# The branch to the general assignment moves from the middle of the program to its end, and redoes the second MoE there

## The chip, the cores and the metric

The kernel runs on one core of one Trainium2 chip. The metric is the device time of one execution in microseconds. The core's engines are PE (TensorE matmuls; PEld is its weight load), DVE (VectorE), ACT (ScalarE), POOL (GpSimd) and SP (SyncE, which issues most DMAs); each runs its own instruction list, and they wait for each other by semaphores. A q behind a name (DVEq) is the engine's sequencer, which also takes the branches.

## What is computed

Three layers follow one another on 1,536 tokens of 512 numbers: attention, an MoE in which every expert sees every token with gates from Sinkhorn sweeps, and a second MoE in which each token goes to one expert:

```python
def _moe2_ref(x, w_gate, w1, w2):
    N, D = x.shape                       # 1536, 512
    E = w_gate.shape[1]                  # 8
    cap = N // E                         # 192
    logits = x @ w_gate
    order = np.argsort(-logits.flatten())
    assigned = -np.ones(N, dtype=np.int64)
    counts = np.zeros(E, dtype=np.int64)
    for idx in order:
        tok, e = (int(idx) // E, int(idx) % E)
        if assigned[tok] >= 0 or counts[e] >= cap:
            continue
        assigned[tok] = e
        counts[e] += 1
    out = np.zeros((N, D), dtype=np.float32)
    for e in range(E):
        mask = assigned == e
        out[mask] = np.maximum(x[mask] @ w1[e], 0.0) @ w2[e]
    return out
```

## The kernel before

Tokens lie on the 128 partitions in twelve tiles. Every product is made of parts: a weight is split into a high and a low half (w1hs and w1ls, w2hs and w2ls; ACT copies the high half, L891, DVE subtracts it for the low one, L889), an activation too (hh and hl). SP loads raw weights (w1r at L867, w2r at L872) into a few buffers, and a load waits until the split has freed its buffer.

The order on each engine is written by a planner, `Sched`: a task has an engine, a cost, dependencies, a priority and buffers or PSUM banks that it takes and gives back; `sch.run()` emits the instructions in the planned order, and the hardware then waits for data alone.

Of the first MoE the last sweeps matter here. `make_gate2` works out the second MoE's gate from the weights of the first: SP loads the gate matrix (wgb) and, block by block, w2 of the last expert (w2f, L1478, two buffers); DVE multiplies them (L1483, 64 products that write the tile junk and keep a sum). Beside it, `zero_rows` (L1466 to L1468) has SP write zeros from junk, which POOL has cleared (L1470), to the first 192 rows of xs_d, the DRAM tensor that the tokens are sorted into.

`make_routing` then assigns tokens by rounds, on DVE, PE and ACT, gives every token a row number (pos) and a flag, flagi, that is 1 if the rounds did not reach the assignment of the reference. With the inputs timed here it is 0. `scatter(t)` on POOL (L1910, L1911) writes the token rows of tile t to xs_d by an indirect DMA, 128 rows of 513 words (512 numbers and the token's index). Ten tiles go first, eight of them from acc, two from accl; the last two tiles, which the first MoE finishes last, go later, and expert 0, whose rows are read before that, gets them by one-hot matmuls instead (slot and hot, L1986 and L1990; the matmuls are L2028).

`general()` stands between the ten scatters and everything that reads xs_d:

```python
            rv = nc.values_load(flagi[0:1, 0:1], min_val=0, max_val=1)
            with tc.If(rv > 0):
                for rnd in range(E - 1):
                    choose(rnd == 0)
                    exact_rank()
```

All five engines load the flag (L1819) and branch (L1820) over the exact assignment and a new set of scatters. It is at that place on each engine's list, so what stands behind it, deferred matmuls of the first MoE (L1090), splits and loads, comes after the branch on its engine.

The second MoE then goes expert by expert (`make_rows`, `make_tr`, `make_step2`): SP loads the expert's rows (xs, L1953), PE transposes them (L2021), multiplies by w1 (L2062 to L2064) and by w2 (L2106 to L2115), ACT and DVE make ya and yb (L2128 to L2135), and `put` (L2138, L2139) on POOL writes them to the output by an indirect DMA with the token's index; there are 16 puts. L206 is a planned filler matmul, L2265 the end of the program.

Of the kernel before, what the change touches and what calls it, by code (L numbers as in the profile page):

```python
# [22 lines left out]
def tile_attention_moe_moe(ctx, tc, q, k, v, n_sink, window, wg1, w1a, w2a, wg2, w1b, w2b, out):  # L23
    nc = tc.nc
# [1418 lines left out]
    def make_gate2():  # L1443
# [3 lines left out]
        def g0():  # L1447
            pool = gctx.enter_context(tc.tile_pool(name="gp", bufs=1, side="right", reuse_waits="tile"))
            gp.update(pool=pool, wgb=pool.tile([P, E, DM], F32, name="wgb"), junk=pool.tile([P, DM], F32, name="junk"),
                      wgt=pool.tile([E, DM], F32, name="wgt"), wgd=dram.tile([E, DM], F32, name="wgd"))  # L1450
            for c in range(DC):
                nc.tensor.transpose(bank["wgt"][:E, c * P:(c + 1) * P], wgr[:, 1, c, :], ident)
# [13 lines left out]
        def zero_rows():  # L1466
            nc.sync.dma_start(xs_d[0:P, 0:DM], gp["junk"])
            nc.sync.dma_start(xs_d[P:cap, 0:DM], gp["junk"][:cap - P])  # L1468

        x = task("POOL", 0.5, lambda: nc.gpsimd.memset(gp["junk"], 0.0), deps=[wgb], prio=pr)  # L1470
# [144 lines left out]
    def make_routing():  # L1615
        pr = -1000.0

        def open_():
            gctx.close()
            pool = rctx.enter_context(tc.tile_pool(name="rt", bufs=1, side="right", reuse_waits="tile"))  # L1620
            for nm, shape, dt in (("V", [P, NT, E], F32), ("A", [P, NT, E], F32), ("K", [P, NT], F32), ("OH", [P, NT, E], F32),
# [5 lines left out]
                                  ("Kr", [P, NT, P], F32), ("S3", [P, 3, NT, E], F32), ("R3", [P, 3, E], F32), ("tv", [P, 3, E], F32),  # L1627
                                  ("T1", [P, NT, E], F32), ("T2", [P, NT, E], F32), ("mxd", [P, NT], F32),
                                  ("Gd", [P, NT, P], BF), ("Gq", [P, P], BF),
# [187 lines left out]
        def general():  # L1817

            rv = nc.values_load(flagi[0:1, 0:1], min_val=0, max_val=1)  # L1819
            with tc.If(rv > 0):  # L1820
                for rnd in range(E - 1):
                    choose(rnd == 0)
                    exact_rank()
                choose(False)
                p = spare()
                rank(p)
                place(p)
                earlier = [o.ins.name for o in sc]
                sc.clear()
                z = rt["Kr"].rearrange("p a b -> p (a b)")[:, :DM]  # L1830
                nc.vector.memset(z, 0.0)
                fill = [nc.gpsimd.dma_start(xs_d[0:P, 0:DM], z), nc.gpsimd.dma_start(xs_d[P:cap, 0:DM], z[:cap - P])]
                for t in range(NE):
                    scatter(t)
                for a, b in [(f, o) for f in fill for o in earlier] + [(sc[0], f.ins.name) for f in fill]:
                    tc.add_manual_dep(a.ins, b, mybir.DependencyInfo(mybir.DependencyClass.Sync, mybir.DependencyReason.DATA),
                                      reason="the rows are written again")

# [59 lines left out]
        return task("X", 0.0, general, deps=SCT + [flag], name="general")  # L1898

    def make_last_scatters():  # L1900
        for t in range(NE, NT):
            SCT.append(task("POOL", 1.1, lambda t=t: scatter(t), deps=[gen, CB[t]] + LDX[0], prio=t, name="scatter"))
# [41 lines left out]
    def make_rows(e, sw):  # L1944
# [11 lines left out]
        LDX[e].append(task("SP", 1.1, ldx, deps=SCT + [sw, gen], prio=v_two(8 * e - 26.0) - (500 if e == 0 else 0), use=[XSH[e]], name=f"xs{e}"))  # L1956

    def make_tr(e):
# [22 lines left out]
        if e == 0:  # L1981
# [11 lines left out]
            hots = {t: task("DVE", 0.2, lambda t=t: hot(t), deps=[h0, gen], prio=-900.0, name="hot") for t in range(NE, NT)}  # L1993
# [53 lines left out]
    def make_step2(s):  # L2047
# [89 lines left out]
        def put(j):  # L2137
# [3 lines left out]
                in_=tl["ya" if j == 0 else "yb"], in_offset=None)  # L2141
# [75 lines left out]
    def more_banks2():  # L2217
        sch.names.extend(("hp0", "hp1"))
        sch.banks.extend([gen.end] * 2)
# [5 lines left out]
    gen = make_routing()  # L2225
    task("X", 0.0, more_banks2, deps=[gen], name="banks")
    sw2 = make_switch2(DEF + [gen])
# [8 lines left out]
    assert not sch.held and made[0] == len(loads)  # L2236

# [32 lines left out]
```

## Time and profile before

| | us |
|---|---|
| median of 3 runs | 1367.23 (1365.68 to 1368.32) |
| the profiled execution's own time | 1365.38 |
| its span, first to last instruction | 1363.6 |
| PE busy in it | 1347.4 (99%) |
| DVE, ACT, POOL busy | 918.0, 610.9, 97.7 |
| mean granted clock of TensorE | 0.998 |

The rows further down come from this one execution; times are us from its first instruction unless marked ns. In a timeline row stand the start, the duration, the engine, the line, the operation, what it writes and reads, and in brackets the idle time of the engine ahead of it with what ended it; a row may group several instructions (x2). In the waits, the engine that waited stands left of the arrow, what it waited for right of it. The time from a DMA's issue to its landing is counted from the issuing instruction to the last byte's arrival. The granted clock (PEclk) is 1.00 at full speed.

### The profile page before, as it was taken

Reading aid. Unit: us, or ns where it says so; the run is one execution under the profiler, and the core shown is the slowest. Engines: PE = TensorE matmul, PEld = TensorE weight load, DVE = VectorE, ACT = ScalarE, POOL = GpSimd, SP = SyncE. Lnnn points to the kernel's source line nnn. Section 1 sums busy time; section 2 is a strip of 40 time slices with the busy share of each in tenths; the row PEclk is TensorE's granted clock in tenths of the full one; section 3 lists DMA queues with packets and bytes.
Section 4 is the critical chain, followed back from the end, with each engine's and each line's share of the span. In section 5 each row is a group of like instructions: output and inputs, shape, how many; then the busy total and the mean of one; then the engine's idle time right before and its main releaser. Section 6 shows DMA issues by size and latency. Waiting matters only on the chain. (4 is left out here: it accounts for less than half of the span.)

```text
span 1363.6 us, 22464 instructions
## 1 busy us (share of the span) xinstructions
PE 1347.4 (99%) x8301; PEld 1171.6 (86%) x8301; DVE 918.0 (67%) x2445; ACT 610.9 (45%) x1543; POOL 97.7 (7%) x238
## 2 busy tenths in 40 slices
PE   8999999999999999999999999999999999899998
PEld 8988888999988888899989888888887777688887
DVE  8877767866555555646364655449889968578885
ACT  7867753734333332424242333331133354267874
POOL 3111110000000000000000000000001023410111
PEclk9999999999999999999999999999999999999999
DMA  7322101201010101011020201061020010478772
GB/s 171 102 63 51 46 17 54 72 22 63 11 52 17 47 19 44 31 32 52 11 62 1 63 4 59 24 216 36 16 93 16 1 47 17 119 231 255 259 225 99
DMA packets 98529, 96.23 MB, mean 71 GB/s; under 512 B 42088, under 2 KB 76392, under 8 KB 98288
## 3 DMA queue, kind: packets, MB, share of 16 engines
q1 hardware_dynamic: 96432, 88.46, 21.8%
q0 software_dynamic: 1984, 6.30, 1.5%
q8 instruction: 66, 1.08, 0.3%
q14 instruction: 47, 0.39, 0.1%
HBM read 86.47 MB, written 8.28 MB: 69 GB/s over the span
## 5 line engine op out<-in xcount | busy, mean ns | idle before, releaser
L1366 ACT ACTIVATE hh<-c 128x256 fp32r<-128x256 f32 x180 | 74.8, 416 | 124.5 <-DVE c L1333 111.0
L1155 PE MATMUL hp<-xp,w1hs 128*128 128x512 f32 x384 | 120.8, 395 | 0.0
L1333 DVE TENSOR_TENSOR c<-hp,cp 128x256 f32<-128x256 f32 x120 | 50.9, 424 | 96.1 <-PE hp L1308 92.7
L1397 PE MATMUL o<-w2ls,hh 128*128 128x512 f32 x240 | 95.0, 396 | 0.0
L1397 PE MATMUL o<-w2hs,hh 128*128 128x512 f32 x240 | 94.4, 393 | 0.0
L1397 PE MATMUL o<-w2hs,hl 128*128 128x512 f32 x240 | 94.4, 393 | 0.0
L1308 PE MATMUL hp<-xp,w1hs 128*128 128x256 f32 x480 | 88.1, 282 | 0.0
L1155 PEld LDWEIGHTS hp<-xp,w1hs 128*128 128x128 f32 x384 | 69.5, 188 | 14.9
L1369 DVE SCALAR_TENSOR_TENSOR hl<-c,hh 128x256 fp32r<-128x256 f32 x180 | 74.5, 419 | 10.4 <-ACT hh L1366 7.8
L1308 PEld LDWEIGHTS hp<-xp,w1hs 128*128 128x128 f32 x480 | 76.6, 188 | 4.6
L1155 PE MATMUL hp<-xp,w1ls 128*128 128x512 f32 x192 | 75.8, 395 | 0.0
L1059 PE MATMUL hp<-xp,w1hs 128*128 128x256 f32 x384 | 74.5, 288 | 0.0
L1090 PE MATMUL o<-w2hs,hh 128*128 128x512 f32 x168 | 68.7, 409 | 4.2 <-PEq L1820 4.2
L1366 ACT ACTIVATE hh<-hp 128x256 fp32r<-128x256 f32 x60 | 23.1, 384 | 107.1 <-PE hp L1308 107.1
L1572 POOL TENSOR_TENSOR hl<-h,hh 128x256 fp32r<-128x256 f32 x15 | 12.9, 863 | 795.8 <-ACT hh L1569 792.1
L1325 ACT ACTIVATE cu<-hp 128x256 f32<-128x256 f32 x60 | 23.0, 383 | 102.7 <-PE hp L1308 102.6
L1308 PE MATMUL hp<-xp,w1ls 128*128 128x256 f32 x240 | 67.5, 281 | 0.0
L1090 PE MATMUL o<-w2ls,hh 128*128 128x512 f32 x168 | 67.0, 399 | 0.0
L1090 PE MATMUL o<-w2hs,hl 128*128 128x512 f32 x168 | 66.5, 396 | 0.0
L1369 DVE SCALAR_TENSOR_TENSOR hl<-hp,hh 128x256 fp32r<-128x256 f32 x60 | 25.4, 424 | 58.7 <-ACT hh L1366 58.4
L889 DVE TENSOR_TENSOR w1ls<-w1r,w1hs 128x512 fp32r<-128x512 f32 x84 | 57.1, 686 | 9.8 <-ACT w1hs L891 9.0
L889 DVE TENSOR_TENSOR w2ls<-w2r,w2hs 128x512 fp32r<-128x512 f32 x84 | 56.0, 683 | 9.3 <-DVEq L1820 6.4
(497 smaller groups left out, 4017.7 us busy)
## 6 DMA issues: line engine op xcount, KB each, us to landing
wr<-in_moe_w_dram SPq DMA_DIRECT2D x44, 512.0 KB, 3.6
w1r<-in_moe_w_dram SPq DMA_DIRECT2D x42, 512.0 KB, 4.6
w2r<-in_moe_w_dram SPq DMA_DIRECT2D x42, 512.0 KB, 4.2
xs<-xs_d SPq DMA_DIRECT2D x14, 256.5 KB, 4.2
nk<-in_k_dram SPq DMA_DIRECT2D x12, 256.0 KB, 3.3
nq<-in_q_dram SPq DMA_DIRECT2D x12, 256.0 KB, 3.8
nv<-in_v_dram SPq DMA_DIRECT2D x12, 256.0 KB, 3.2
wgb<-wgd SPq DMA_DIRECT2D x1, 2048.0 KB, 8.9
```

The source lines that it names most:

```text
L889: (nc.gpsimd if eng == "POOL" else nc.vector).tensor_tensor(lo[:, c], r[:, c], f32(hi[:, c]), op=OP.subtract)
L1059: nc.tensor.matmul(p, a, b, start=(c == 0 and j == 0), stop=(c == DC - 1 and j == 2), skip_group_check=True)
L1090: nc.tensor.matmul(OUTP[g, j], a_, b_, start=(first and i == 0), stop=(last and i == 2), skip_group_check=True)
L1155: nc.tensor.matmul(HS[k, 0].rearrange("p a b -> p (a b)"), a, b, start=(c == 0 and j == 0), stop=(c == DC - 1 and j == 2), skip_group_chec ...
L1308: nc.tensor.matmul(st[bk], l_[:, c], r_[:, c], start=(start and c == 0 and j == 0), stop=(c == 1 and j == 2), skip_group_check=True)
L1325: act(st[key], st[bk], AF.Copy)
L1333: tt(st[out], st[bk], st[key], op=OP.add)
L1366: act(hh, st[key], AF.Relu)
L1369: nc.vector.scalar_tensor_tensor(HT[i, f, t][1], st[key], 0.0, f32(HT[i, f, t][0]), op0=OP.max, op1=OP.subtract)
L1397: nc.tensor.matmul(OUTP[g, j % GT], a_, b_, start=(first and f == 0 and z == 0), stop=(last and f == 1 and z == 2), skip_group_check=True)
L1572: (nc.gpsimd if eng == "POOL" else nc.vector).tensor_tensor(HT[s][1], h32_of(g, fc), f32(HT[s][0]), op=OP.subtract)
```

## The change

`general()` is no longer a task of the plan. It is called once, after `sch.run()`, behind the last instruction of every engine, and its body now does the exact assignment, twelve scatters, and the whole second MoE again in a plain loop. The rest of the program no longer depends on it: the last scatters, xs and hot depend on `placed` (the row numbers), and the banks hp0 and hp1 come back to the planner when the first MoE's last H32 tasks end instead of when the branch does. Since the second MoE now runs ahead of the branch even where the rounds failed, rows of xs_d that no token was sorted into must be harmless: all 1,536 rows are filled from a tile of their own (zero) with zeros and the index N, in twelve DMAs, and `put` has a bounds check that drops rows with the index N.

```diff
+                      wgt=pool.tile([E, DM], F32, name="wgt"), wgd=dram.tile([E, DM], F32, name="wgd"),
+                      zero=pool.tile([P, XW], F32, name="zero"))
...
         def zero_rows():
-            nc.sync.dma_start(xs_d[0:P, 0:DM], gp["junk"])
-            nc.sync.dma_start(xs_d[P:cap, 0:DM], gp["junk"][:cap - P])
-
-        x = task("POOL", 0.5, lambda: nc.gpsimd.memset(gp["junk"], 0.0), deps=[wgb], prio=pr)
+            for j in range(NT):
+                nc.sync.dma_start(xs_d[j * P:(j + 1) * P, :], gp["zero"])
+
+        def zero():
+            nc.gpsimd.memset(gp["zero"][:, :DM], 0.0)
+            nc.gpsimd.memset(gp["zero"][:, DM:], float(N))
+
+        x = task("POOL", 0.5, zero, deps=[wgb], prio=pr)
...
-        return task("X", 0.0, general, deps=SCT + [flag], name="general")
+        rt.update(choose=choose, exact_rank=exact_rank, rank=rank, place=place, spare=spare)
+        return place_, flag
 
     def make_last_scatters():
         for t in range(NE, NT):
-            SCT.append(task("POOL", 1.1, lambda t=t: scatter(t), deps=[gen, CB[t]] + LDX[0], prio=t, name="scatter"))
+            SCT.append(task("POOL", 1.1, lambda t=t: scatter(t), deps=[placed, CB[t]] + LDX[0], prio=t, name="scatter"))
+
+    def general():
+
+        choose, exact_rank, spare = rt["choose"], rt["exact_rank"], rt["spare"]
...
+        rv = nc.values_load(flagi[0:1, 0:1], min_val=0, max_val=1)
+        with tc.If(rv > 0):
...
+            for rnd in range(E - 1):
+                choose(rnd == 0)
+                exact_rank()
...
+            for t in range(NT):
+                scatter(t)
+            for e in range(E):
...
-        LDX[e].append(task("SP", 1.1, ldx, deps=SCT + [sw, gen], prio=v_two(8 * e - 26.0) - (500 if e == 0 else 0), use=[XSH[e]], name=f"xs{e}"))
+        LDX[e].append(task("SP", 1.1, ldx, deps=SCT + [sw, placed], prio=v_two(8 * e - 26.0) - (500 if e == 0 else 0), use=[XSH[e]], name=f"xs{e}"))
...
-                in_=tl["ya" if j == 0 else "yb"], in_offset=None)
+                in_=tl["ya" if j == 0 else "yb"], in_offset=None, bounds_check=N - 1, oob_is_err=False)
...
-        sch.banks.extend([gen.end] * 2)
+        sch.banks.extend([max(x.end for x in B_HP)] * 2)
...
     sch.run()
     assert not sch.held and made[0] == len(loads)
+    general()
```

On every engine the order of the other instructions is the same as before, apart from the names of PSUM banks in the routing and the zero rows. What moves is the load of the flag, the branch, and the body that is jumped over. The body has, in rows of the instruction order, before and now: PE about 2,300 and 900, DVE 407 and 771, ACT 23 and 312, POOL 25 and 61, SP 2 and 83.

**At the old place of the branch, SP.** Before (w1r and w2r are raw weights, xs the rows of expert 0):

```order
L867 DMA w1r<-in_moe_w_dram 128x4x256 x5
L1819 TENSOR_LOAD flagi
L1819 ISA x2
L1820 COMPARE_AND_BRANCH
L1820 UNCONDITIONAL_BRANCH x2
L872 DMA w2r<-in_moe_w_dram 128x2x512 x2
L1953 DMA xs_14661<-xs_d 128x512
L1953 DMA xs_14663<-xs_d 64x512
L872 DMA w2r<-in_moe_w_dram 128x2x512 x2
```

Now the w2r load that stood behind the branch follows the last w1r load directly:

```order
L867 DMA w1r<-in_moe_w_dram 128x4x256 x5
L872 DMA w2r<-in_moe_w_dram 128x2x512 x2
L2021 DMA xs_12972<-xs_d 128x512
L2021 DMA xs_12974<-xs_d 64x512
L872 DMA w2r<-in_moe_w_dram 128x2x512 x2
```

The flag's load and the branch are gone from this place; the order of the loads is kept.

**At the old place of the branch, PE.** Before (o and av are PSUM banks, hh and hl the halves of an activation of the first MoE; L1871 is the first row of the body):

```order
L1090 MATMUL av<-w2ls_130,hh 128x512
L1090 MATMUL o_12879<-w2hs_129,hl 128x512
L1090 MATMUL av<-w2hs_129,hl 128x512
L1819 TENSOR_LOAD flagi
L1820 COMPARE_AND_BRANCH
L1871 MATMUL hp_12938<-ident,rK 128x128 x4
L1871 MATMUL hp_12944<-ident,rK 128x128 x4
L1871 MATMUL hp_12950<-ident,rK 128x128 x4
```

Now the matmuls that stood behind the body follow directly, in the same order, into banks of other names:

```order
L1090 MATMUL side_12889<-w2ls_130,hh 128x512
L1090 MATMUL hp_12884<-w2hs_129,hl 128x512
L1090 MATMUL side_12889<-w2hs_129,hl 128x512
L1090 MATMUL hp_12884<-w2hs_129,hh 128x512
L1090 MATMUL side_12889<-w2hs_129,hh 128x512
L1090 MATMUL hp_12884<-w2ls_130,hh 128x512
L1090 MATMUL side_12889<-w2ls_130,hh 128x512
```

On DVE it is the same: behind the two hl (L1572) there stood the flag's load and the branch, and now the split of w2r into w2ls (L889) and the next two hl follow.

**At the end, DVE.** Now (yb is the last tile of the second MoE, and ended DVE's list before; L1899 is the first row of the new body):

```order
L2156 SCALAR_TENSOR_TENSOR hs<-sm,hs 128x128
L2157 SCALAR_TENSOR_TENSOR hs<-sm,hs 128x64
L2203 TENSOR_TENSOR yb<-av,yb 64x512
L1897 TENSOR_LOAD flagi
L1898 COMPARE_AND_BRANCH
L1899 CAST gonesb<-ones 128x128
L1900 CAST gbefb<-before 128x128
```

The flag's load and the branch stand behind yb, and likewise behind the last instruction of every other engine.

**At the zero rows, SP.** Before:

```order
L1478 DMA w2f<-in_moe_w_dram 128x512
L1467 DMA xs_d<-junk 128x512
L1468 DMA xs_d<-junk 64x512
L1478 DMA w2f<-in_moe_w_dram 128x512
L872 DMA w2r<-in_moe_w_dram 128x2x512
L867 DMA w1r<-in_moe_w_dram 128x4x256
```

Now:

```order
L1483 DMA w2f<-in_moe_w_dram 128x512
L1469 DMA xs_d<-zero 128x513 x12
L1483 DMA w2f<-in_moe_w_dram 128x512
L872 DMA w2r<-in_moe_w_dram 128x2x512
L867 DMA w1r<-in_moe_w_dram 128x4x256
```

The twelve DMAs stand where the two stood, ahead of the second w2f load.

## Rows read from the trace of the kernel before

**Rows 1.** Waits of PE, longest first: us in total, times, longest.
```profile
PE o L1090 <- PEq L1820: 4.2, 1, 4.2
```

**Rows 2.** Line L1820, the branch, by engine: duration ns, first and last start.
```profile
L1820 ACTq COMPARE_BRANCH  x1: 50/50/50, 1181.1 to 1181.1; - x1
L1820 ACTq EVENT_SEMAPHORE  x1: 17/17/17, 1181.6 to 1181.6; - x1
L1820 DVEq COMPARE_BRANCH  x1: 72/72/72, 1182.1 to 1182.1; - x1
L1820 DVEq EVENT_SEMAPHORE  x1: 21/21/21, 1187.8 to 1187.8; - x1
```

**Rows 3.** Line L1819, the load of the flag, on DVE.
```profile
L1819 DVEq TENSOR_LOAD <-flagi x1: 803/803/803, 1181.2 to 1181.2; - x1
```

**Rows 4.** Timeline of PE at the branch: start us, us, what; idle before it.
```profile
1182.04 0.39 PE L1090 MATMUL av<-w2hs,hl 128*128 128x512 f32 x1
...
1186.66 0.47 PE L1090 MATMUL o<-w2hs,hh 128*128 128x512 f32 x1 [4.23 <-PEq L1820]
...
1190.62 0.39 PE L1090 MATMUL o<-w2hs,hl 128*128 128x512 f32 x1
...
1195.29 1.52 PE L2021 MATMUL side<-ident,xs 128*128 128x128 f32 x8
```

**Rows 5.** Windows: busy us (xcount) of PE, PEld, DVE, ACT, POOL; PEclk, DMA share, GB/s.
```profile
1186.66:1190.62 3.96, 3.96 (x11) 3.11 (x12) 2.62 (x7) 1.46 (x3) 0.33 (x2) 0.57 0.10 19
...
1201.80:1355.70 153.90, 153.25 (x887) 135.11 (x886) 125.58 (x342) 110.62 (x268) 18.46 (x28) 1.00 0.70 224
```

**Rows 6.** Timeline of SP around the branch.
```profile
1173.46 16.22 SPq L872 DMA_DIRECT2D w2r<-in_moe_w_dram  x2
1189.79 0.98 SPq L1953 DMA_DIRECT2D xs<-xs_d  x2
```

**Rows 7.** Timeline of POOL: the tenth scatter, and what waits for its landing.
```profile
1180.99 0.96 POOL L1911 DMA_INDIRECT xs_d<-accl,pos  x1 [0.21 <-POOLq L1820]
1189.63 0.29 POOL L1986 IOTA slot<- 128x192 f32 x1 [7.68 <-DMA xs_d<-acc,pos]
```

**Rows 8.** DMA issues, us to landing: first four scatters, all scatters, then the row loads.
```profile
xs_d<-acc,pos POOLq DMA_INDIRECT x4, 5.1
...
DMA to landing us min/median/max: 3.8/5.9/9.0
...
DMA to landing us min/median/max: 2.7/3.0/4.9
```

**Rows 9.** Windows, columns as in the fifth group: loads, and the scatters.
```profile
915.00:920.00 5.00, 5.00 (x23) 4.02 (x22) 2.25 (x7) 0.58 (x2) 0.00 (x0) 1.00 0.94 281
...
1170.00:1182.30 12.30, 12.30 (x55) 9.71 (x53) 5.91 (x18) 4.50 (x11) 10.03 (x18) 1.00 0.84 218
```

**Rows 10.** SP's second load of w2f: its issue, and its us to landing.
```profile
905.53 0.79 SPq L1478 DMA_DIRECT2D w2f<-in_moe_w_dram  x1
...
w2f<-in_moe_w_dram SPq DMA_DIRECT2D x1, 256.0 KB, 12.7
```

**Rows 11.** Timeline of DVE at the gate products (L1483) and next to them.
```profile
918.17 0.69 DVE L1483 SCALAR_TENSOR_TENSOR junk<-w2f,wgb 128x512 f32<-128x512 f32 x1 [2.23 <-DMA xs_d<-junk]
...
924.58 0.69 DVE L1483 SCALAR_TENSOR_TENSOR junk<-w2f,wgb 128x512 f32<-128x512 f32 x1
...
927.40 0.75 DVE L1178 SCALAR_TENSOR_TENSOR hl<-hp,hh 128x256 fp32r<-128x256 f32 x2
```

**Rows 12.** Timeline of PE: the matmul that first takes that hl.
```profile
931.20 0.39 PE L1090 MATMUL o<-w2hs,hl 128*128 128x512 f32 x1
```

**Rows 13.** Timeline of DVE and POOL at the end, and POOL's last drain (L2265).
```profile
1357.99 0.68 DVE L2135 TENSOR_TENSOR yb<-o,yb 64x512 f32<-64x512 f32 x1 [2.87 <-ACT yb L2132]
1358.95 0.90 POOL L2139 DMA_INDIRECT out_dram<-yb,idx  x1 [0.28 <-DVE yb L2135]
...
L2265 POOLq DRAIN  x3: 40/113/4022, 1358.7 to 1363.3; - x3
```

More of the change, by code (lines that the diff above doesn't have):

```diff
@@ L1449, in g0 @@
             gp.update(pool=pool, wgb=pool.tile([P, E, DM], F32, name="wgb"), junk=pool.tile([P, DM], F32, name="junk"),
-                      wgt=pool.tile([E, DM], F32, name="wgt"), wgd=dram.tile([E, DM], F32, name="wgd"))
+                      wgt=pool.tile([E, DM], F32, name="wgt"), wgd=dram.tile([E, DM], F32, name="wgd"),
+                      zero=pool.tile([P, XW], F32, name="zero"))
             for c in range(DC):
@@ L1626, in open_ @@
                                   ("mk", [P, E], F32), ("fl", [P, 4], F32), ("posf", [P, NT], F32),
-                                  ("Kr", [P, NT, P], F32), ("S3", [P, 3, NT, E], F32), ("R3", [P, 3, E], F32), ("tv", [P, 3, E], F32),
-                                  ("T1", [P, NT, E], F32), ("T2", [P, NT, E], F32), ("mxd", [P, NT], F32),
-                                  ("Gd", [P, NT, P], BF), ("Gq", [P, P], BF),
+                                  ("T1", [P, NT, E], F32), ("T2", [P, NT, E], F32),
                                   ("bte", [P, NT, E], F32), ("far", [P, NT], F32)):
@@ L1815, in make_routing @@
         place_ = task("DVE", 0.9, lambda: place(bank["rk"]), deps=[y], prio=pr - 1, rel="rk")
[L1817 to L1837, printed above, removed]
         sp_n = [0]
@@ L1992, in make_tr @@
             h0 = task("POOL", 0.3, hot0, deps=[sw2], prio=-900.0)
-            hots = {t: task("DVE", 0.2, lambda t=t: hot(t), deps=[h0, gen], prio=-900.0, name="hot") for t in range(NE, NT)}
+            hots = {t: task("DVE", 0.2, lambda t=t: hot(t), deps=[h0, placed], prio=-900.0, name="hot") for t in range(NE, NT)}
         for c2 in range(DC // 2):
@@ L2224, in tile_attention_moe_moe @@
         make_deferred(q_)
-    gen = make_routing()
-    task("X", 0.0, more_banks2, deps=[gen], name="banks")
-    sw2 = make_switch2(DEF + [gen])
+    placed, flag = make_routing()
+    B_HP = list(H32.values())
+    task("X", 0.0, more_banks2, deps=B_HP, name="banks")
+    sw2 = make_switch2(DEF + [placed, flag])
     for e in range(E):
```

74 lines of the change are left out of this document (added).

## The prediction, made before the changed kernel ran

> **What bounds the kernel now.** PE is busy for nearly the whole span (the table above), so whatever makes the program shorter must take idle or slow time from PE, or time from the tail behind its last matmul. I read the list of PE's waits first. Its longest is at the branch of L1820, 4.2 us, once [rows 1]. The view of that line by engine tells who stood there: DVE branches at 1182.1 and goes on at 1187.8, while ACT branches at 1181.1 and goes on at 1181.6 [rows 2]. Both skip the same body, of which DVE has 407 rows in the instruction order and ACT 23. So the stall goes with the length of what is jumped over; it isn't the load of the flag, which took DVE 0.8 us of its own ahead of the branch [rows 3]. PE's timeline shows the whole price [rows 4], the windows show that PE came back at a granted clock of 0.57, the 1.2 GHz level for most of it, for 3.96 us, and that the second MoE behind it is PE's again: 153.25 us busy of 153.90 [rows 5]. A microsecond saved ahead of it therefore reaches the end, unless PE waits for something else on the way.
>
> **The branch leaves the middle: −6.0 us.** From the last matmul ahead of the branch to the next one are 1186.66 − 1182.04 = 4.62 us [rows 4]. From 1190.62 to 1195.29, 20 matmuls take 4.67 us, 0.2335 us each, so 4.39 us of the 4.62 are idle. The ten matmuls from 1186.66 to 1190.62 take 3.96 us instead of 2.34: 1.62 us of slow clock. Together 6.0. PE can then begin the transposes of expert 0's rows (L2021 of before) at 1195.29 − 6.0 = 1189.3.
>
> **What is late next: +1.0 us.** These transposes read xs of expert 0, which SP loads from xs_d behind the tenth scatter's landing; that dependency stays. Before, the tenth scatter was issued at 1180.99, and POOL's iota, which waited for its landing, started at 1189.63, and SP's first xs load at 1189.79 [rows 6, 7]: a landing near 1189.1, 8.1 us after the issue. Scatters of this kernel land in 3.8 to 9.0 us, median 5.9; the first four, median 5.1 [rows 8]. The first w2r load behind the branch was issued at 1173.46 [rows 6], into the middle of the scatters. In the changed order it follows the last w1r load with no flag load between, so it goes long before the scatters and its bytes are out of the way, and I take 5.1: a landing at 1186.1. The second w2r load waits for the DVE split (L889), which stood behind DVE's branch and now runs from about 1181.7; it is out by about 1183 and may cost the scatters a little. With 0.7 us from landing to the first xs issue, as before, 0.5 us more to the second, and 3.0 us to land (median [rows 8]), xs is there at 1190.3, 1.0 us after PE is ready. Bounds: a landing after 3.8 us and a load of 2.7 gives 1188.7, no wait; a landing at 1189.1 as before and a load of 4.9 us gives 1195.2, a wait of 5.9.
>
> **The zero rows: +0.2 us.** Two DMAs of 128 and 64 rows of 2,048 bytes become twelve of 128 rows of 2,052 bytes: 3.15 MB for 0.39 MB, 2.76 MB more, at the same place of SP's queue, just ahead of the second w2f load. They are issued while weights are loading: the queue runs at 281 GB/s at a DMA share of 0.94 [rows 9]. By that rate the extra bytes take 9.8 us. The w2f load landed at 905.53 + 12.7 = 918.2 [rows 10], and would now at 928.0; DVE needs it at 924.58 [rows 11], so it is 3.4 us late. The cover: the hl that DVE makes behind the first four products from it is done at 927.40 + 0.75 = 928.15, and PE takes it at 931.20 [rows 12], 3.05 us later. That leaves 0.4 by this sum. DVE is no longer held by the zero DMAs before its first product (2.23 us idle there [rows 11]; junk is no longer their source), which puts it a little ahead; I take 0.2. Bounds: 0, and at the 218 GB/s of the scatters' window [rows 9] 12.7 us, that is 6.3 late and 3.3 on PE. Twelve issues of at most 0.79 us each [rows 10] are 9.5 us on SP; they lie within the same stretch. If the cover were gone, the price would be the 3.4 us.
>
> **The branch at the end: +1.4 us.** Each engine now loads the flag and branches after its last instruction, over a longer body (PE 900 rows, DVE 771, ACT 312, SP 83, POOL 61). PE and ACT, for which DVE's last instruction waits, and SP, whose last load is older still, have these beside DVE's. DVE's last instruction, yb, starts at 1357.99 [rows 13]. In the middle its flag load started at 1181.2, while its last instruction still ran, and it went on at 1187.8 [rows 2, 3], 6.6 us; the same from 1358.05 gives 1364.7. With PE's stall of 4.39 in place of DVE's 5.7 it is 1363.3. Before, POOL's drain ended at 1358.72 + 4.02 = 1362.7, and the span 0.8 later at about 1363.6 [rows 13]. So DVE adds 0.6 to 1.9, POOL's own load and branch run while the last put is landing, and I take 1.4. Bounds: 0.1 if the fetch is quicker on an idle DMA; 4.3 if POOL also has to fetch after its last put's issue at 1359.85. POOL's body in the middle was 25 rows and showed no stall of its own that can be told from its wait for the scatter; 61 is nearer to ACT's 23 without a stall than to DVE's 407 with one, so I take none.
>
> A rule bears on this. The Trainium skill, page "Runtime: NRT & Kernel Launch", section "Instruction fetch mechanics", says that instructions are fetched ahead strictly in sequence, in blocks of 256, two held at a time, and that a taken branch out of them makes the engine wait for a fetch. The trace agrees for ACT and DVE [rows 2]. By the rule ACT with 312 rows would now stall too, but off the path, and POOL with 61 would not, which leaves the sum at the −3.4 below; where POOL's branch lies near a block's edge, it is the −0.5 of the third rival.
>
> The bounds check on the 16 puts: no row shows it; the puts lie beside PE except the last, so 0 to 0.5, taken as 0. The PSUM banks that come back earlier change names in the routing, no engine's order: 0.
>
> **Sum.** −6.0 + 1.0 + 0.2 + 1.4 = −3.4 us. The profiled execution took 1365.38 us (span 1363.6), 1.85 below the median of 1367.23; so 1362.0 for it, and 1363.8 against the median.
>
> **Rivals.**
> 1. *The row load takes the branch's place.* If the tenth scatter still lands at 1189.1 (HBM writes, not w2r, were what it stood behind), xs lands at 1193.3 with a load of 3.0 us, PE waits 4.0, and 1.6 us of slow clock follow as behind the old stall. −6.0 + 5.6 + 0.2 + 1.4 = +1.2: 1368.4, and with a load of 4.9 us +3.1. For it: POOL already waited 7.68 us for that landing [rows 7]. Against it: the first four at 5.1. It decides from a landing after about 1187.
> 2. *Zero rows hold the gate products: slower than before.* At 218 GB/s the second w2f lands at 930.9; PE idles 3.3 us near 931 and pays 1.6 of clock: −3.4 − 0.2 + 4.9 = +1.3, 1368.5. It decides from a w2f landing later than 924.58 + 3.05 = 927.6, that is below 290 GB/s. For it: 281 is just under that. Against it: the rows written are long and from one tile, and DVE gets its start earlier.
> 3. *A fetch on POOL at the end.* +4.3 in place of 1.4: −0.5, 1366.7.
> 4. *The stall isn't the branch's* (it comes from what stands behind it, such as the code of the second MoE): then nothing is gained and the end and the zero rows pay, +1.6, 1368.8.
>
> **Chances.** Forecast 0.60; rivals 0.16, 0.11, 0.08, 0.05. A measurement of this kernel can tell about 0.2%, 2.7 us, from no change: 1364.5 to 1370.0 is "same". The forecast case runs from −6 (no wait, no zero cost) to −1.5 and is below −2.7 in most of its weight, 0.50 of 0.60; with 0.02 of the others, faster is 0.52. The far ends of rivals 1 and 2 and what they make together are slower: 0.11. Same is 0.37. Range: the low end is −6.0 + 0.2 = −5.8, 1361.4; the high end takes in rival 3 and the near side of 1, 2 and 4, 1368.3.
>
> **What the profile would show.** Right: PE's list of waits has no PEq entry in the middle; the window before the transposes has a clock of 1.00; the second xs load lands near 1190, with PE waiting about a microsecond for it; PE near 931 is gapless; DVE's branch at the end holds it for some 4 to 5.7 us, with the last event near 1365 on a scale from which 4.8 is taken. Wrong: a wait of 3 us or more at the transposes with a clock near 0.57 behind it (rival 1); DVE waiting for w2f after 924.6 and PE for hl near 931 (rival 2); POOL's event more than 2 us behind its put's landing (rival 3); the middle stall at the same place without a branch (rival 4).

## The result: the changed kernel is slower by 0.9%

| | before | changed |
|---|---|---|
| median of 6 runs, us | 1367.97 (1365.68 to 1369.73) | 1379.57 (1377.68 to 1382.10) |
| ratio, 95% interval | | 1.0087 (1.0073 to 1.0101) |
| span of the profiled execution | 1363.6 | 1375.5 |
| mean granted clock | 0.998 | 0.992 |

The forecast was 1363.8, range 1361.4 to 1368.3. The direction is wrong and the time lies outside the range. (The kernel before is measured here on six runs, 1367.97; the prediction was made against three of them, 1367.23.)

In the changed kernel the stall at the old place of the branch [rows 1] is gone. Two other waits stand in PE's list instead (us in total, times, longest):

```profile
PE o L1090 <- DVE hl L1178: 6.7, 1, 6.7
...
PE side L2089 <- DMA xs<-xs_d: 2.1, 2, 1.2
```

The first is near 931 us. SP's timeline there: the twelve zero DMAs kept SP for 17.6 us, and the second w2f load went out at 924.06 in place of 905.53 [rows 10].

```profile
905.83 17.61 SPq L1469 DMA_DIRECT2D xs_d<-zero  x12
924.06 0.33 SPq L1483 DMA_DIRECT2D w2f<-in_moe_w_dram  x1
```

DVE's timeline: the first product from that block started at 936.34, after 12.19 us of waiting; before, it started at 924.58 [rows 11].

```profile
936.34 0.69 DVE L1488 SCALAR_TENSOR_TENSOR junk<-w2f,wgb 128x512 f32<-128x512 f32 x1 [12.19 <-DMA w2f<-in_moe_w_dram]
```

PE's timeline: the matmul that takes the hl behind it waited for 6.72 us; before it ran without a wait [rows 12].

```profile
932.52 0.40 PE L1090 MATMUL o<-w2ls,hh 128*128 128x512 f32 x1
939.64 0.79 PE L1090 MATMUL o<-w2hs,hl 128*128 128x512 f32 x1 [6.72 <-DVE hl L1178]
```

The windows (columns as in rows 5) show the queue behind the last issue of zeros: 132 and 141 GB/s at DMA shares of 1.10 and 1.11 from 925 to 935, where before there were 281 at 0.94 while the weights were loading [rows 9]. They also show three stretches with PE busy at about half the clock: behind this wait, and behind the second one.

```profile
925.00:930.00 5.00, 5.00 (x24) 4.03 (x23) 0.00 (x0) 0.66 (x2) 0.00 (x0) 1.00 1.10 132
930.00:935.00 5.00, 2.92 (x13) 2.02 (x11) 0.00 (x0) 0.66 (x2) 0.00 (x0) 1.00 1.11 141
...
940.00:943.10 3.10, 3.10 (x9) 2.37 (x9) 2.96 (x9) 0.00 (x0) 0.00 (x0) 0.54 0.01 5
...
1202.30:1206.00 3.70, 3.70 (x12) 2.76 (x12) 1.29 (x2) 1.15 (x2) 2.11 (x4) 0.50 0.83 269
1206.00:1210.00 4.00, 4.00 (x16) 3.88 (x17) 0.00 (x0) 0.05 (x1) 0.00 (x0) 0.61 0.29 80
```

The second wait is at the transposes of expert 0's rows. POOL's timeline has the tenth scatter at 1190.94, SP's the first xs load behind its landing at 1197.81, 6.87 us later (8.80 before [rows 6, 7]):

```profile
1190.94 0.96 POOL L1979 DMA_INDIRECT xs_d<-accl,pos  x1 [0.22 <-issue]
```

```profile
1197.81 0.91 SPq L2021 DMA_DIRECT2D xs<-xs_d  x2
```

PE had the last deferred matmul at 1198.99 and could have gone on 0.23 later. It waited twice, and the first matmul of the second MoE came at 1211.19. Where the clock is 1.00 that stretch takes 6.5 us from the first transposes [rows 4, 5]; here it took 10.61.

```profile
1198.99 0.40 PE L1090 MATMUL side<-w2hs,hl 128*128 128x512 f32 x1
1200.58 0.49 PE L2089 MATMUL side<-ident,xs 128*128 128x128 f32 x2 [1.18 <-DMA xs<-xs_d]
1201.97 1.77 PE L2089 MATMUL side<-ident,xs 64*128 64x64 f32 x6 [0.91 <-DMA xs<-xs_d]
...
1211.19 0.42 PE L2130 MATMUL side<-xe,w1hs 128*128 128x384 f32 x1
```

At the end, the last matmul starts at 1366.02, so the span ends 9.48 us behind it (called the tail below). Before, it started at 1356.78, and the tail was 6.82. The two rows, before and changed:

```profile
1356.78 0.40 PE L2115 MATMUL o<-w2ls,hs 128*64 128x512 f32 x1
1366.02 0.40 PE L2183 MATMUL av<-w2ls,hs 128*64 128x512 f32 x1
```

The branch, by engine (duration in ns min/median/max, first and last start), and POOL's drain behind it:

```profile
L1898 POOLq EVENT_SEMAPHORE  x5: 17/43/2516, 1368.7 to 1371.5; - x5
...
L1898 ACTq COMPARE_BRANCH  x1: 50/50/50, 1367.0 to 1367.0; - x1
L1898 DVEq COMPARE_BRANCH  x1: 72/72/72, 1367.9 to 1367.9; - x1
...
L1898 ACTq EVENT_SEMAPHORE  x1: 17/17/17, 1369.4 to 1369.4; - x1
L1898 DVEq EVENT_SEMAPHORE  x1: 21/21/21, 1371.2 to 1371.2; - x1
L1898 POOLq INC_SWDGE_SEM  x1: 730/730/730, 1371.6 to 1371.6; - x1
```

```profile
L2335 POOLq DRAIN  x3: 40/107/2352, 1372.4 to 1375.3; - x3
```

DVE branches at 1367.9 and is back at 1371.2. POOL waits until 1371.5 (its last put, issued at 1368.19, took 3.2 us to land), spends 0.73 us on INC_SWDGE_SEM, read here as its queue's bookkeeping, and only then drains for 2.35 us. Before, the drain ran beside the landing [rows 13].

Put together, by the starts of the same instructions in the two traces (SP's wgb load, POOL's first scatter, PE's first matmul of the second MoE, its last matmul, the end). The rows that stand nowhere else, before (with PE's last deferred matmul) and then changed:

```profile
902.96 0.35 SPq L1456 DMA_DIRECT2D wgb<-wgd  x1
1168.71 1.17 POOL L1911 DMA_INDIRECT xs_d<-acc,pos  x1 [0.29 <-DVE rinc L1763]
1195.06 0.40 PE L1090 MATMUL av<-w2hs,hl 128*128 128x512 f32 x1
1201.80 0.42 PE L2062 MATMUL side<-xe,w1hs 128*128 128x384 f32 x1
```

```profile
904.41 0.35 SPq L1457 DMA_DIRECT2D wgb<-wgd  x1
1178.65 1.17 POOL L1979 DMA_INDIRECT xs_d<-acc,pos  x1 [0.30 <-DVE rinc L1766]
```

| stretch | before | changed | difference |
|---|---|---|---|
| start to the wgb load | 902.96 | 904.41 | +1.45 |
| wgb load to first scatter (zero rows in it) | 265.75 | 274.24 | +8.49 |
| first scatter to first matmul of the second MoE | 33.09 | 32.54 | −0.55 |
| from there to the last matmul | 154.98 | 154.83 | −0.15 |
| last matmul to the end | 6.82 | 9.48 | +2.66 |

The sum is +11.9, the difference of the spans. The third row is −6.01 up to the last deferred matmul (20.34 us from the first scatter in place of 26.35) and +5.46 behind it.

### The profile page after: what moved, and what is told of

Its sections match the earlier page's. It is cut to its first block, busy times and chain, and to the rows that moved or that the text cites. A ratio compares the mean times of both kernels' runs of the same rounds, so it can differ in the third digit from the quotient of the medians.

```text
span 1375.5 us, 22493 instructions
## 1 busy us (share of the span) xinstructions
PE 1352.8 (98%) x8301; PEld 1176.1 (86%) x8301; DVE 918.0 (67%) x2445; ACT 610.9 (44%) x1543; POOL 98.0 (7%) x239
## 4 chain that ended last, share of the span: by engine, by line
PE 92%; DMA 4%; DVE 1%; POOL 1%; ACT 1%; issue 1%; SPq 0%; POOLq 0%; ACTq 0%; DVEq 0%
PE hp L1308 15%; PE o L1397 12%; PE o L1090 9%; PE hp L1155 8%; PE side L1308 6%; PE side L1397 6%; PE av L1397 6%; PE hp L1059 5%; PE side L1090 2%; PE av L683 2%; PE side L2130 2%; PE o L206 1%; PE av L1090 1%; PE side L660 1%; DMA xs_d<-zero 1%; DMA w1r<-in_moe_w_dram 1%
## 5 line engine op out<-in xcount | busy, mean ns | idle before, releaser
L1397 PE MATMUL o<-w2ls,hh 128*128 128x512 f32 x240 | 95.0, 396 | 0.0
L1397 PE MATMUL o<-w2hs,hh 128*128 128x512 f32 x240 | 94.4, 393 | 0.0
L1397 PE MATMUL o<-w2hs,hl 128*128 128x512 f32 x240 | 94.4, 393 | 0.0
L1155 PEld LDWEIGHTS hp<-xp,w1hs 128*128 128x128 f32 x384 | 69.5, 188 | 15.0
L1308 PEld LDWEIGHTS hp<-xp,w1hs 128*128 128x128 f32 x480 | 76.6, 188 | 4.6
L1090 PE MATMUL o<-w2hs,hl 128*128 128x512 f32 x176 | 70.1, 398 | 6.7 <-DVE hl L1178 6.7
L1090 PE MATMUL o<-w2hs,hh 128*128 128x512 f32 x176 | 72.2, 410 | 0.0
L1366 ACT ACTIVATE hh<-hp 128x256 fp32r<-128x256 f32 x60 | 23.1, 384 | 107.1 <-PE hp L1308 107.1
L1090 PE MATMUL o<-w2ls,hh 128*128 128x512 f32 x176 | 70.4, 400 | 0.0
L1175 ACT ACTIVATE hh<-hp 128x256 fp32r<-128x256 f32 x48 | 16.9, 383 | 107.0 <-PE hp L1155 105.1
L889 DVE TENSOR_TENSOR w1ls<-w1r,w1hs 128x512 fp32r<-128x512 f32 x84 | 57.1, 685 | 9.7 <-ACT w1hs L891 9.0
L1059 PEld LDWEIGHTS hp<-xp,w1hs 128*128 128x128 f32 x384 | 60.1, 188 | 2.5 <-DVE xp L716 0.2
```

Source lines behind the costliest of these rows:

```text
L889: (nc.gpsimd if eng == "POOL" else nc.vector).tensor_tensor(lo[:, c], r[:, c], f32(hi[:, c]), op=OP.subtract)
L1059: nc.tensor.matmul(p, a, b, start=(c == 0 and j == 0), stop=(c == DC - 1 and j == 2), skip_group_check=True)
L1090: nc.tensor.matmul(OUTP[g, j], a_, b_, start=(first and i == 0), stop=(last and i == 2), skip_group_check=True)
L1155: nc.tensor.matmul(HS[k, 0].rearrange("p a b -> p (a b)"), a, b, start=(c == 0 and j == 0), stop=(c == DC - 1 and j == 2), skip_group_chec ...
L1308: nc.tensor.matmul(st[bk], l_[:, c], r_[:, c], start=(start and c == 0 and j == 0), stop=(c == 1 and j == 2), skip_group_check=True)
L1366: act(hh, st[key], AF.Relu)
```

## The experiments

Theory: zero rows +8.5, late rows of expert 0 with the half clock behind them +5.5, POOL's end +2.7, and the branch itself −6.0 as forecast. Ratios are to the kernel before on the same chip. The stretches are those of the table above.

| run | ratio (95%) | wgb to scatter | scatter to second MoE | last matmul to end |
|---|---|---|---|---|
| zero_only | 1.0062 (1.0040 to 1.0084) | 273.38 | 31.20 | 6.80 |
| after_two | 1.0038 (1.0020 to 1.0056) | 265.59 | 33.37 | 9.55 |
| after_spread | 1.0043 (1.0027 to 1.0059) | 265.61 | 33.10 | 9.87 |
| after_noend | 1.0085 (1.0062 to 1.0108) | 273.52 | 31.61 | 6.80 |
| spread_swap | 1.0017 (1.0007 to 1.0027) | 266.26 | 32.50 | 9.50 |
| swap_noend | 0.9997 (0.9985 to 1.0008) | 265.70 | 32.55 | 6.76 |
| spread_xs | 1.0013 (0.9998 to 1.0027) | 265.55 | 32.76 | 10.49 |
| spread_xs_fill | 1.0000 (0.9990 to 1.0009) | 265.61 | 28.66 | 10.20 |
| spread_fill | 0.9995 (0.9983 to 1.0007) | 265.52 | 33.02 | 9.71 |
| fill_noend | 0.9977 (0.9964 to 0.9989) | 265.46 | 28.41 | 6.72 |
| zero_align | one execution, no ratio | 265.60 | 30.51 | 10.13 |
| zero_2048 | one execution, no ratio | 272.32 | 32.10 | 9.88 |
| zero_pitch | one execution, no ratio | 265.43 | 30.97 | 10.28 |
| end_nopool | one execution, no ratio | 274.03 | 32.45 | 7.44 |

**The zero rows alone.** In the kernel before, `zero_rows` and the tile `zero` as in the change, nothing else:

```diff
-            nc.sync.dma_start(xs_d[0:P, 0:DM], gp["junk"])
-            nc.sync.dma_start(xs_d[P:cap, 0:DM], gp["junk"][:cap - P])
+            for j in range(NT):
+                nc.sync.dma_start(xs_d[j * P:(j + 1) * P, :], gp["zero"])
```

> The kernel before, with one part of the change alone: the twelve DMAs of zero rows (128x513) from a tile of their own, at the same place; the branch stays in the middle. Theory (the zero rows hold the second w2f load, DVE waits for it, PE waits for DVE's hl and comes back at half the clock): slower than before by about 8.5 us (6.9 of wait, 1.6 of clock), PE waits 6 to 7 us for hl near 931, DVE 12 us for w2f. Rival (the wait near 931 comes from something else of the change, as the freed banks or the tile's place in SBUF): within 1 us of before, no such wait.

It was 0.62% slower, 8.5 us of 1363.84, with PE waiting 6.0 us for hl. DVE's row:

```profile
933.86 0.69 DVE L1488 SCALAR_TENSOR_TENSOR junk<-w2f,wgb 128x512 f32<-128x512 f32 x1 [11.42 <-DMA w2f<-in_moe_w_dram]
```

The theory holds. The same kernel has the branch in the middle, and there PE's wait at it was 2.3 us in that execution, not 4.2: DVE branched at 1189.5 and went on at 1192.5, 3.0 us for the body that cost it 5.7 in the trace of the kernel before.

**Only two of them, in the changed kernel.**

```diff
-            for j in range(NT):
-                nc.sync.dma_start(xs_d[j * P:(j + 1) * P, :], gp["zero"])
+            nc.sync.dma_start(xs_d[0:P, 0:DM], gp["zero"][:, :DM])
+            nc.sync.dma_start(xs_d[P:cap, 0:DM], gp["zero"][:cap - P, :DM])
```

> The changed kernel with only the first 192 rows filled, by two DMAs as before (from the new tile). Left out: the zeros and the index N in the other 1,344 rows, which only matter where the assignment by rounds fails. Theory: 8.5 us faster than the changed kernel, about 3 us slower than before (what is left of it: +2.7 at the end, -0.5 in the middle); no wait of PE for hl near 931. Rival: the twelve DMAs cost only part, and a wait of some us stays near 931.

The stretch is 265.59 again and the wait near 931 is gone. The ratio's interval, 2.7 to 7.6 us over before, holds the 3 us that were expected. Against the changed kernel's 1.0087 it is 0.49% better, 6.7 us, where 8.5 were expected; the two intervals together leave room for that.

**All twelve, spread.** The loop of twelve and the planner's dependency on it are taken out (not shown); in its place:

```diff
+            if 1 <= c <= NT // 2:
+                for j in (2 * c - 2, 2 * c - 1):
+                    ZR.append(task("SP", 1.5, lambda j=j: zero_rows(j), deps=[x, done[-1]], prio=pr + 10.0 * c + j, name="zero"))
```

> The changed kernel with the twelve zero DMAs spread, two at a time, behind the gate products of the second to the seventh w2f block (about 930 to 960), where the trace shows a DMA share of 0.11 to 0.20. Theory (it is their place ahead of the second w2f load, with the loads of other weights in flight, that costs): about as fast as with two DMAs, 8.5 us faster than the changed kernel. Rival (3.1 MB of such writes cost wherever they lie, since each two hold the next w2f load): a wait of DVE for w2f at several blocks, and less than half of the 8.5 us come back.

265.61: spread over 931 to 969 us (two by two, the last four together) the same 3.15 MB cost nothing in this stretch. It is their place and their being together that cost.

**What makes the burst slow.** Three kernels write the burst at its old place with other rows. `zero_align`: rows past 192 go to a tensor of their own, 2,048 bytes each without gaps. `zero_2048`: into the sorted tensor, 2,048 bytes of each 2,052. `zero_pitch`: again a tensor of their own, 2,052 bytes at a pitch of 2,112. In the first and the third the first 192 rows go to the sorted tensor by two DMAs, as in `after_two`. The edits, in this order:

```diff
-            for j in range(NT):
-                nc.sync.dma_start(xs_d[j * P:(j + 1) * P, :], gp["zero"])
+            nc.sync.dma_start(xs_d[0:P, 0:DM], gp["zero"][:, :DM])
+            nc.sync.dma_start(xs_d[P:cap, 0:DM], gp["zero"][:cap - P, :DM])
+            xz = dram.tile([NT * P, DM], F32, name="xz")
+            for j in range(2, NT):
+                nc.sync.dma_start(xz[j * P:(j + 1) * P, :], gp["zero"][:, :DM])
```

```diff
-                nc.sync.dma_start(xs_d[j * P:(j + 1) * P, :], gp["zero"])
+                nc.sync.dma_start(xs_d[j * P:(j + 1) * P, :DM], gp["zero"][:, :DM])
```

```diff
-            for j in range(NT):
-                nc.sync.dma_start(xs_d[j * P:(j + 1) * P, :], gp["zero"])
+            nc.sync.dma_start(xs_d[0:P, 0:DM], gp["zero"][:, :DM])
+            nc.sync.dma_start(xs_d[P:cap, 0:DM], gp["zero"][:cap - P, :DM])
+            xz = dram.tile([NT * P, XW + 15], F32, name="xz")
+            for j in range(2, NT):
+                nc.sync.dma_start(xz[j * P:(j + 1) * P, :XW], gp["zero"])
```

> The changed kernel with the zeros of the rows past 192 written in rows of 2,048 bytes to a DRAM tensor of their own, ten DMAs of 128x512, at the same place. Left out: these rows of the sorted tensor stay unfilled. Theory A (a burst of 3 MB of writes in the middle of weight loads is slow whatever its rows are): the second w2f still lands 15 us or more later than before, PE waits 5 to 7 us for hl. Theory B (rows of 2,052 bytes, which begin off a 64-byte border, make the writes slow): the burst goes at the 281 GB/s or more of the loads, w2f lands within 10 us of before, and PE waits under 1 us.

> The changed kernel with twelve zero DMAs of 128x512 into the same rows of 2,052 bytes' pitch (left out: the column with the index N). Each row written is 2,048 bytes long and begins off a 64-byte border for most rows. Theory (the border): as slow as the changed kernel, PE waits 5 us or more for hl near 931. Rival (the 4 bytes more in each row): as fast as with rows of 2,048 bytes in a tensor of their own, no wait of PE there.

> The changed kernel with the zeros of the rows past 192 written as rows of 2,052 bytes into a tensor of their own with a pitch of 2,112 bytes, so that each begins on a 64-byte border (left out: these rows of the sorted tensor stay unfilled). Theory (the border and the shared blocks between neighbouring rows make the burst slow): as with aligned rows of 2,048 bytes, PE waits under 1 us for hl near 931. Rival (the odd length does): the second w2f lands 12 us or more later than before, and PE waits 4 us or more.

DVE's first product from the second w2f block in `zero_2048`, `zero_align` and `zero_pitch`, in this order:

```profile
934.02 0.69 DVE L1488 SCALAR_TENSOR_TENSOR junk<-w2f,wgb 128x512 f32<-128x512 f32 x1 [9.79 <-DMA w2f<-in_moe_w_dram]
```

```profile
925.92 0.69 DVE L1491 SCALAR_TENSOR_TENSOR junk<-w2f,wgb 128x512 f32<-128x512 f32 x1 [1.75 <-DMA w2f<-in_moe_w_dram]
```

```profile
927.66 0.69 DVE L1491 SCALAR_TENSOR_TENSOR junk<-w2f,wgb 128x512 f32<-128x512 f32 x1 [3.52 <-DMA w2f<-in_moe_w_dram]
```

Rows at a pitch of 2,048 or 2,112 bytes, both multiples of 64, leave PE without a wait there. Rows of 2,048 bytes at the old pitch of 2,052 made it wait 4.3 us for hl, less than the 5 that were expected and than the 6.7 of the changed kernel. So the length of the row is at most a part of it. The two fast kernels share the pitch, but also that ten of their DMAs go to another tensor than xs_d. The runs do not tell these two apart; that the pitch does it is the likelier reading, and not shown, and neither is why a border of 64 bytes should matter. Each of the three ran once.

SP was held in the fast kernels too. Its rows in `zero_align` and then `zero_pitch`:

```profile
907.09 13.91 SPq L1472 DMA_DIRECT2D xz<-zero  x10
921.04 0.62 SPq L1486 DMA_DIRECT2D w2f<-in_moe_w_dram  x1
```

```profile
907.35 13.28 SPq L1472 DMA_DIRECT2D xz<-zero  x10
920.68 0.45 SPq L1486 DMA_DIRECT2D w2f<-in_moe_w_dram  x1
```

The second w2f load went out only 3.0 and 3.4 us earlier than in the changed kernel, but DVE's product from it started 4.9 and 7.0 us after that issue in place of 12.3. Most of the gain is thus in the queue behind the issue, not in the time that SP was held.

**The end taken away.**

```diff
     assert not sch.held and made[0] == len(loads)
-    general()
```

> The changed kernel without the call behind the plan: no load of the flag, no branch, no body at the end (left out: the general assignment). Theory (POOL's branch puts the wait for the last put's landing and the queue's bookkeeping ahead of its drain): 2.7 us faster than the changed kernel, and the tail from PE's last matmul to the end is 6.8 us as before in place of 9.5. Rival (the tail is longer because of the bounds check or of the larger program): no gain, the tail stays at 9.5.

The tail is 6.80 again, by the trace 2.7 us less. The `put` with the bounds check is still in this kernel, so that isn't what lengthens the tail. The ratio can't confirm the gain by itself: it is 0.02% better than the changed kernel's, and its interval is as wide as the effect. Between `spread_swap` and `swap_noend`, and between `spread_xs_fill` and `fill_noend`, each pair with this one difference, it is 0.20% and 0.23%.

The same trace has one short wait of PE at expert 0's transposes:

```profile
1199.92 1.81 PE L2089 MATMUL side<-ident,xs 128*128 128x128 f32 x8 [0.94 <-DMA xs<-xs_d]
```

From there the first matmul of the second MoE took 9.92 us to come, in place of 6.5, at granted clocks of 0.78, 0.50 and 0.69: 3.4 us of slow clock behind 0.94 us of wait, where 1.6 followed the old stall of 4.2. Why the longer stall cost less is not shown.

**A body without POOL.** The scatters and the puts of the body are gone, the rest stays.

```diff
-            sc.clear()
-            for t in range(NT):
-                scatter(t)
...
-                for y, i in zip((ya, yb), ix):
-                    nc.gpsimd.memset(spacer, 0.0)
-                    nc.gpsimd.indirect_dma_start(out=out, out_offset=bass.IndirectOffsetOnAxis(ap=i[:, :1], axis=0), in_=y,
-                                                 in_offset=None)
```

> The changed kernel with a body at the end that has no instruction on POOL (left out: the scatters and the puts of the general assignment). DVE still jumps over as many rows. Theory (POOL, whose queue's landings and bookkeeping have to be settled where its body is skipped, ahead of its drain, sets the end): the tail from PE's last matmul to the end falls from 9.5 to about 7 us. Rival (DVE's stall at the branch, 3.3 us, sets it): it stays above 9.

The tail fell to 7.44. POOL's last drain starts early again and lies beside the landing, while DVE comes back as late as in the changed kernel (5.2 us behind the start of PE's last matmul in both):

```profile
L2328 POOLq DRAIN  x3: 40/113/3947, 1368.1 to 1372.6; - x3
...
L2328 DVEq DRAIN  x2: 10/14/17, 1370.8 to 1372.4; - x2
```

So what POOL settles sets the end, and DVE's stall is beside it (one execution).

**The w2r load behind xs.** With the zero rows spread as above, one w2r load is emitted after expert 0's xs loads; the plan is otherwise left as it is. (The end of the line is left out at the dots, and so is the emission from the list `late` behind the xs loads.)

```diff
-            return task("SP", 1.46, l2, deps=deps + [d1] + ...
+            return task("SP", 1.46, (lambda: late.append(l2)) if need - n_defer == 2 else l2, deps=deps + [d1] + ...
```

> The changed kernel with the zero DMAs spread (as in the run before) and one w2r load on SP moved from ahead of expert 0's xs loads to behind them. Theory (that w2r load's bytes stand in front of the tenth scatter's and of xs; the short waits of PE at the transposes then cost 3.4 to 4.5 us of half clock behind them): xs is issued under 5 us after the tenth scatter in place of 5.5 to 6.9, PE waits under 0.5 us at the transposes, the clock stays at 1.00 there, and from the first scatter to the first matmul of the second MoE are 27 to 28 us in place of 33.1; about 5 us faster than with the spread alone, 1 to 3 us faster than before. Rival (the scatters' own landing sets it): the wait stays at 1 to 2 us, with the half clock behind it, and no gain.

A miss. xs was issued 6.04 us after the tenth scatter, not under 5, and the stretch took 32.50 us, not 27 to 28. PE waited 0.5 us for xs, but then 2.2 us for accl, because DVE, which takes its list in order, stood 8.07 us at the split of the load that I had moved:

```profile
1196.26 0.69 DVE L889 TENSOR_TENSOR w2ls<-w2r,w2hs 128x512 fp32r<-128x512 f32 x1 [8.07 <-ACT w2hs L891]
```

```profile
1197.67 1.33 PE L2098 MATMUL side<-hot,accl 128*128 128x192 f32 x3 [2.19 <-DVE accl L1106]
```

The same without the call of `general()`:

> The same without the flag's load, branch and body at the end (left out: the general assignment). Theory: 2.7 us faster than with it, by the tail alone (6.8 us from PE's last matmul to the end in place of 9.5 to 9.9), 4 to 6 us faster than before. Rival (the code behind the plan costs something elsewhere, or nothing): the tail differs by under 1 us, or the rest of the span moves too.

As expected in the tail (6.76) and the rest; 0.9997 instead of 4 us better, since the middle had not been mended.

**The same by the planner.** The changed part of the line alone, zero rows spread as above:

```diff
-(SCT[NE - 1:NE] if 1 <= need - n_defer < 3 else [])
+(SCT[NE - 1:NE] if need - n_defer == 1 else LDX[0] if need - n_defer == 2 else [])
```

> As in the run where the w2r load was moved behind expert 0's xs loads, but by the planner (the load depends on them), so that the splits that need it are planned later too, behind the last accl on DVE. Theory (in the run before, the wait of 2.2 us for accl was the moved load's: DVE and ACT take their list in order, and the split of w2r stood ahead of accl): no wait of PE for accl, a wait of 0.5 to 1 us for xs; the half clock behind it, if it comes, is all that is left, and from the first scatter to the first matmul of the second MoE are 28 to 31 us. Rival (accl is late for its own reasons): the wait for accl stays.

The wait for accl is gone; the stretch is 32.76, beyond the 28 to 31 that were expected. xs was still issued 6.90 us after the tenth scatter, without the load in its way, so my theory that the w2r load makes the difference falls: over the profiles of the kernels with no branch in the middle this time is 5.0 to 8.1 us with the load ahead of xs and 4.9 to 6.9 with it behind. A smaller part of it isn't ruled out. The clock behind two short waits (1.3 and 0.9 us) was 0.65 and 0.62:

```profile
1191.90:1195.70 3.80, 3.80 (x14) 2.88 (x14) 1.17 (x2) 1.15 (x2) 2.12 (x4) 0.65 0.78 284
1195.70:1201.20 5.50, 5.50 (x24) 5.46 (x24) 0.84 (x3) 1.24 (x3) 0.00 (x0) 0.62 0.55 182
```

**Dummy transposes in the wait.**

```diff
+                    for _ in range(12):
+                        nc.tensor.transpose(bank[key][:, :P], ident, ident)
```

> The same with twelve dummy transposes of the identity on PE ahead of expert 0's transposes (1.3 us at full clock), where PE otherwise waits for xs. Theory (it is the idle microsecond that brings the clock to half, and that costs 3.4 to 4.5 us, more than the wait): no idle time there, the clock stays at 1.00, 28 us from the first scatter to the first matmul of the second MoE (33.1 before, 32.5 in the changed kernel), and 1 to 3 us faster than before over the whole. Rival (the clock falls whatever PE does there, or the transposes only come on top): 1.3 us slower than without them.

PE goes from the twelve transposes into expert 0's without idle time, and the clock stays at 1.00 over the stretch (compare the 0.65 and 0.62 above):

```profile
1189.18 1.47 PE L2086 MATMUL side<-ident 128*128 128x128 f32 x12
1190.51 0.49 PE L2091 MATMUL side<-ident,xs 128*128 128x128 f32 x2
```

```profile
1189.10:1197.30 8.20, 8.14 (x55) 7.12 (x52) 3.47 (x6) 2.44 (x6) 2.11 (x4) 1.00 0.69 234
```

28.66 us in place of 32.76. The whole kernel is as fast as the one before, 1.0000; I had expected 1 to 3 us more, and the tail of 10.20 and a new wait of PE for the rows of expert 1 (1.4 us) took them.

The same transposes in the kernel with spread zero rows alone, the w2r load where the change has it:

> The changed kernel with spread zero rows and the twelve dummy transposes, the w2r load left where the change has it (ahead of xs). Theory A (the scatters' own landing sets xs, the w2r load's place is of no account): as fast as with the load moved, within 1 us, and xs is issued 6 to 7 us after the tenth scatter as there. Theory B (the load's bytes stand in the way): xs lands later, PE waits 0.5 us or more behind the transposes and the clock falls, 2 us or more slower.

By the times the place of the w2r load makes no difference (0.9995 against 1.0000), as theory A says. The profiled execution, the second slowest of the twelve, reads as theory B says: xs issued 8.07 us after the scatter, a wait of 1.2 us behind the transposes and the clock down again, 33.02. That would fit twelve being enough in some executions only; which executions, and whether the load has a part in it, stays open.

And `spread_xs_fill` without the call of `general()`:

> The kernel with spread zero rows, the w2r load planned behind expert 0's xs loads and twelve dummy transposes, without the flag's load, branch and body at the end (left out: the general assignment). Theory (the tail is the last of the change's costs, and the sum of the parts is the whole): 2.7 to 3.4 us faster than with the end, so 3 us faster than the kernel before, tail 6.8 us. Rival (the parts don't add): within 1 us of the kernel before.

0.9977, 3.1 us faster than before: the parts add up. This kernel has no fallback; a whole one that beats the kernel before was not found. A body that does without POOL's DMAs might be what is missing; it was not run together with the other two mends.

## Why the prediction was wrong, step by step

- **The branch leaves the middle, −6.0: right for this pair of executions.** From the first scatter to the last deferred matmul it is 20.34 us in place of 26.35. In `zero_only`, with the same branch still in the middle, that stretch took 24.46 us: by that trace the branch cost 4.1. So the agreement to the tenth is in part luck.
- **What is late next, +1.0: mis-sized, it was +5.46.** The wait was 2.1 us: the tenth scatter's rows were there after 6.8 us, not the 5.1 that I took from the first four, and the reason that I gave for the old 8.1 (a w2r load in the middle of the scatters) did not hold: `zero_only` still has that load there, at 1181.00, and issued xs 6.13 us after its tenth scatter. The larger part, 3.4 us, is a price that I left out: I had charged slow clock to the old stall of 4.2 us, and none to a wait of 1 to 2 us. The trace shows 0.50 and 0.61, the 1.2 GHz level for most of it, over nearly 8 us behind it, and the dummy transposes show that the idle time did it. Rival 1 had the mechanism and priced its clock at 1.6.
- **The zero rows, +0.2: the step that failed, it was +8.49.** I let 2.76 MB more go at the 281 GB/s of a stretch with loads in it, so that the second w2f load would come 9.8 us later. No row showed a burst of stores like these: at its end the queue moved 132 to 141 GB/s. With the rows of `zero_align` the same load was 6.0 us late (its later start of 1.67 taken off), within my price, so the rate was wrong for these rows and not for any burst. And I called SP's twelve issues 9.5 us beside other work: they held SP for 17.6 us, and the second w2f load stood behind them on SP's list. DVE's first product from it came 11.76 us later than before, 10.3 with the 1.45 of the start taken off; the cover of 3.05 leaves 7.3, and PE lost 6.9 and 1.6 of clock. Rival 2 had this mechanism, with 0.11 and a price of 4.9; its bound, the 218 GB/s of the scatters, allowed 12.7 us for a load that came 16.7 us late (again without the 1.45), so it was no bound.
- **The branch at the end, +1.4: mis-sized, +2.66, and for another reason.** DVE's stall was 3.3 us, less than the 4.4 to 5.7 that I took, and lay beside POOL's work; with that gone (`end_nopool`) the tail is 0.6 us over before, the low end of what I gave DVE. POOL did not stall for code either, so rival 3 did not happen; ACT with 312 rows did now, from 1367.0 to 1369.4, beside DVE. Both agree with the rule in the Trainium skill, page "Runtime: NRT & Kernel Launch", section "Instruction fetch mechanics". But POOL's wait for its DMAs, which I had seen in the middle and had taken for the scatters' landing alone, moved ahead of the drain, with 0.73 us of bookkeeping behind it.
- The start of +1.45 goes with one of the two outcomes told at the end, not with the branch's place. Rival 4, that the stall was not the branch's, did not happen.

## What to carry to other kernels

A stall that is taken away is worth what the next arrival allows, and where that leaves a microsecond or two of idle time on PE, the clock behind it can cost more than the wait (here 3.4 us against 2.1); work that is of no use, put into the wait, can pay for itself. Price stores that are added to a queue by the load that stands behind them on the issuing engine, not by the queue's mean rate, and try rows in DRAM at a pitch that is a multiple of 64 bytes: here such rows, in a tensor of their own, left no wait. Ask of everything that is moved to the end of a program what the engines settle there one after the other.

## What was not expected of the hardware

Behind twelve DMAs of 128 rows at a pitch of 2,052 bytes, among loads, the queue moved 132 GB/s at a DMA share of 1.10, and the engine that issued them was held for 17.6 us. The same rows two to four at a time, at DMA shares of 0.06 to 0.82, cost nothing.

The first 20 us of the program have two outcomes. In ten of the sixteen profiled executions (the changed kernel's among them) the clock fell there, and the wgb load came at 904.4 to 904.8; in the six others (among them that of before) it stayed, and the load came at 902.9 to 903.2. Kernels with the branch at the end show both, so the branch's place does not decide it. That it goes with the execution is likely, but each kernel has one profile, so it is not shown. The window from 10 to 20 us in the changed kernel, and in `spread_xs`:

```profile
10.00:20.00 10.00, 8.01 (x58) 7.75 (x57) 7.83 (x29) 5.99 (x22) 3.68 (x4) 0.83 1.14 246
```

```profile
10.00:20.00 10.00, 8.11 (x75) 7.48 (x72) 9.28 (x35) 6.90 (x25) 3.45 (x3) 1.00 1.07 240
```
